# A hashed-attention kernel with two gated layers: the first head, the last head and the weight conversions dealt anew

## The chip, the cores and the metric

The program runs on one core of a Trainium2 chip. The metric is the time of one execution on the device in microseconds (us). The core has a TensorE (PE; its weight loads are a row of their own, PEld), a VectorE (DVE), a ScalarE (ACT), a GpSimd (POOL), a SyncE (SP) that here only issues DMAs, and DMA queues on SP and ACT. The engines run side by side and wait for each other through semaphores. A difference of over 0.3% of the time (2.2 us) is what a measurement of this kernel can tell.

## The reference, cut to what matters

```python
def _attn_ref(q, k, v, proj):                       # (2, 8, 768, 64) each, proj (64, 6)
    q_bits = (np.einsum('bhsd,dk->bhsk', q, proj) > 0)
    k_bits = (np.einsum('bhsd,dk->bhsk', k, proj) > 0)
    # bucket = sum(bits * 2**arange(6)); mask = q_bucket == k_bucket
    scores = scale * np.matmul(q, k.transpose(0, 1, 3, 2))
    scores = np.where(mask, scores, -1000000000.0)
    scores = scores - np.max(scores, axis=-1, keepdims=True)
    attn = np.exp(scores)
    attn = attn / (np.sum(attn, axis=-1, keepdims=True) + 1e-09)
    return np.matmul(attn, v)
# x = heads side by side, (1536, 512)
def _moe_ref(x, w_in, w_out):                       # w_in (512, 2048), w_out (2048, 512)
    h = x @ w_in
    return (h * np.tanh(np.log1p(np.exp(h)))) @ w_out
def _moe2_ref(x, w_in, w_out, a, b):
    h = x @ w_in
    P = a[0] + a[1] * h + a[2] * h**2 + a[3] * h**3
    Q = 1.0 + abs(b[0]) * abs(h) + abs(b[1]) * h**2
    return (P / (Q + 1e-06)) @ w_out
```

The three functions are applied one after the other. The weights of the two layers come as 64-bit floats, everything else as 32-bit floats.

## The kernel before, in words

**Precision.** Every large product is made from a rounded part ("hi") and a remainder ("lo"): `XH`, `XL`, `W[..][:, 0]`, `W[..][:, 1]`, `gh`, `gl`. A product is three: hi·hi, lo·hi, hi·lo. The lo parts are subtractions on VectorE (L73) or GpSimd (L70), the hi parts copies on ScalarE (L64) or GpSimd (L67).

**Attention.** 16 heads, one after the other, 768 queries by 768 keys, six key blocks `c` of 128. The bucket mask is folded into the score product: rows of codes (L328 to L341) stand under K and Q, and one more row holds each query's maximum. For that row `smax` (L392) multiplies six query blocks by all keys (two matmuls each, L398) and reduces each block on VectorE (L402). For all but head 0 the maxima are then transposed on VectorE (L410) and moved by a DMA of ACT's queue (`qB<-stt`, L415) into a row of `qB`; for head 0 matmuls with an identity (`row0`, L422) and two copies do it. Then `st` (L437) multiplies each key block by all queries (four matmuls, L446) and ScalarE takes the exponential of 128x768 (L451). `pair` (L471) adds exponentials two by two on GpSimd, `pv` multiplies by V (L293, 48 rows of the trace per head) and `dsum` (L481) adds the three sums of pairs with a matrix of ones. Two heads on, the divisors are gathered, inverted and spread by DMAs (L519, L531, L539), `norm` multiplies by them on VectorE (`xf`, L548), and `xhi`, `xlo` split the result for the layers.

**Order of the attention.** Each head has six slots. The table `order` in `attention` says in which slot a function of a head is called and, by the order of its lines, in which order the functions of one slot are; since each engine takes its instructions in program order, this sets the queues. The beginning is written out by hand (`start`). `warm(n)` issues n small matmuls on ones, whose result is not used. `two_banks` hands out four PSUM tiles in turn.

**Weights.** 64-bit floats become 32-bit by three integer operations on VectorE (L103, L106, L109), called a conversion below; then come hi and lo. Seven of the first layer's 16 feature tiles (`EARLY`) are converted during attention, in 14 parts, each split on GpSimd behind its conversion (`slot_split`). The other nine are converted in 36 parts over the steps of the first layer that `C1_AT` gives, and the second layer's later in the first layer; those are stored and read back as 32-bit words, and split from step n1-11 on (`split_at`).

**Dense part.** 96 steps: two layers, three blocks of 512 tokens, 16 feature tiles. A step is `gemm1` of one tile (12 matmuls, L731) and `gemm2` of an earlier one (12 matmuls, L749 or L751, of which four wait for `gl`), with the elementwise work of `front`, `recip`, `last`, `back` between. `tail(i)` puts the attention slots that remain behind the last head into steps 2, 3 and 5. Steps n1 (48) on belong to the second layer. `finish` writes the output, a tile of 128x512 per DMA.

Of the kernel before, what the change touches and what calls it, by code (L numbers as in the profile page):

```python
# [29 lines left out]
OLD = 3  # L30
EARLY = 7
# [7 lines left out]
C1_AT = 1, 14  # L39
# [8 lines left out]
def attention_moe_moe(ctx: ExitStack, tc: tile.TileContext, kq, v, proj2, cst, eye, w1, w2, ab, out):  # L48
# [110 lines left out]
    def attention(actx, tctx):  # L159
# [13 lines left out]
        turn = [0]  # L173
        ahead = []

        def two_banks():
            if ahead:
                return ahead.pop()
            turn[0] += 1
            return T[(turn[0] - 1) % 4]  # L180
# [20 lines left out]
        def memsets():  # L201
# [4 lines left out]
            for t in T:  # L206
                nc.vector.memset(t[:, :, HALF:HALF + 1], -BIG / 4)
# [24 lines left out]
        def load(h):  # L232
# [3 lines left out]
            if h == 0:  # L236
                home[0] = wpool.tile([128, 2, 2 * DM], F32, tag=f"w{EARLY - 1}", name="kq")
            raws[h] = home[0][:, h % 2, 0:S]
            nc.sync.dma_start(out=raws[h], in_=kq[b, hh])


# [17 lines left out]

        def khi(i):  # L260
            o = KK[0][64:128, i] if i < 2 else qX[0][0:64]
            nc.scalar.activation(out=o, in_=raws[0][0:64], func=ACT.Copy)

        def qhi():
            nc.vector.tensor_copy(qB[0][64:128], raws[0][64:128])
# [4 lines left out]
        def klo():  # L270
            lo_pool(qX[0][0:64], raws[0][0:64], qX[0][0:64])
# [42 lines left out]
        def codes(h):  # L314
            if not 0 <= h < OLD:
                return
            p = [two_banks() for _ in range(1 + (h == 0))]
            ct[h] = p[0][:, 0], p[-1][:, 1]
# [3 lines left out]
        def warm(n):  # L322
            if not ahead:
                ahead.append(two_banks())
            for _ in range(n):
                nc.tensor.matmul(out=ahead[0][0:32, 0, 0:128], lhsT=ones, rhs=wones, start=True, stop=True)
# [60 lines left out]
        def signs(h):  # L387
            for a in range(2):
                code_k(h, (a,))
                code_q(h, (1 - a,))  # L390

        def smax(h, c):  # L392
            if not 0 <= h < B * H:
                return
            p = two_banks()
            m = SM[h % 2][:, c:c + 1] if h else Z[:, 32 + c:33 + c]
            for a in range(2):
                nc.tensor.matmul(  # L398
                    out=p[:, a, 0:HALF], lhsT=qB[h % NB][:, c * 128:(c + 1) * 128], rhs=qhalf(KK[h % NB][:, 0], a),
                    start=True, stop=True,  # L400
                )
            nc.vector.tensor_reduce(out=m, in_=p[:, :, 0:HALF + 1], op=ALU.max, axis=AX.XY)  # L402
# [16 lines left out]
        def row0():  # L419
            p = two_banks()  # L420
            for c in range(NC):
                nc.tensor.matmul(  # L422
                    out=p[0:64, c // 3, c % 3 * 128:c % 3 * 128 + 128], lhsT=Z[:, c:c + 64], rhs=I_t,
                    start=True, stop=True,
                )
            nc.vector.tensor_copy(qhalf(qB[0], 1)[32:33], p[32:33, 1, 0:HALF])
            nc.scalar.activation(out=qhalf(qB[0], 0)[32:33], in_=p[32:33, 0, 0:HALF], func=ACT.Copy)
# [8 lines left out]

# [550 lines left out]
```

## Time and profile before

| | |
|---|---|
| time, median of 3 runs | 734.08 us (734.04 to 735.63) |
| the profiled execution | 734.39 us, of it 732.6 from the first instruction to the last |
| PE, PEld busy | 724.3 us (99%), 577.1 us (79%) |
| DVE, ACT, POOL busy | 575.9 us (79%), 416.4 us (57%), 130.3 us (18%) |
| DMA | 82.89 MB, mean 113 GB/s |

Durations in the rows come from that one profiled execution. PE's busy time counts matmuls that run at half the clock, and matmuls overlap, so 99% does not say that nothing could be shorter; what PE waits for stands in the waits and in the stretches. The attention takes the first 204 us, the first dense layer lies from 204 to 470, the second behind it. A row of the timeline joins like instructions of one engine that follow each other; its second number runs from the first one's start to the last one's end.

### The profile page before, as it was taken

The page shows a single profiled execution, that of the slowest core. Times are in us where ns is not written, and L with a number is a line of the kernel's source. Part 1 is how long each engine was busy: PE and PEld are TensorE (multiplying, and loading weights), DVE is VectorE, ACT ScalarE, POOL GpSimd, SP SyncE. Part 2 cuts the span into 40 slices and gives each one's busy share as a digit, 9 for nine tenths or more (in the row PEclk, how much of TensorE's full clock was granted, in tenths as well). Part 3 has the DMA queues.
Part 4 walks back from the last instruction along what each step waited for, and adds up shares of the span by engine and source line. Part 5 has one row for each costly group of instructions (what it writes and reads, how often), then busy time and mean ns, then how long its engine had stood idle before and what let it go on. Part 6 is the DMA issues. An engine that isn't in the chain of part 4 may idle for free.

```text
span 732.6 us, 11610 instructions
## 1 busy us (share of the span) xinstructions
PE 724.3 (99%) x4212; PEld 577.1 (79%) x4212; DVE 575.9 (79%) x1042; ACT 416.4 (57%) x688; POOL 130.3 (18%) x108
## 2 busy tenths in 40 slices
PE   8999999999999999999999999999999999999997
PEld 6777777676778788888888888878888888888886
DVE  6878898988568994655556876599998888898886
ACT  5766767676644432212122334687877767777674
POOL 7657566665700000000000000000000000000000
PEclk9999999999999999999999999999999999999999
DMA  5777868885144442455446884200001000010001
GB/s 156 207 205 191 224 183 215 192 213 141 35 129 137 146 138 78 151 165 172 145 151 203 275 251 156 86 1 1 0 1 57 1 1 0 1 58 0 1 1 58
DMA packets 48505, 82.89 MB, mean 113 GB/s; under 512 B 6634, under 2 KB 24256, under 8 KB 48448
## 3 DMA queue, kind: packets, MB, share of 16 engines
q1 hardware_dynamic: 48123, 82.07, 38.6%
q8 instruction: 33, 0.54, 0.3%
q14 instruction: 25, 0.20, 0.1%
q10 hardware_dynamic: 324, 0.08, 0.1%
HBM read 55.71 MB, written 14.14 MB: 95 GB/s over the span
## 4 chain that ended last, share of the span: by engine, by line
PE 83%; DVE 7%; DMA 5%; issue 1%; ACT 1%; POOL 1%; SPq 0%; POOLq 0%; ACTq 0%; DVEq 0%
PE h L731 31%; PE y L751 17%; PE y L749 15%; PE s L446 7%; PE s L293 6%; PE s L398 4%; PE s L481 1%; DMA d<-rc 1%; DMA qB<-stt 1%; DVE w L73 1%; DVE t L106 1%; DVE r L109 1%; DVE z L402 1%; DVE gl L73 1%; DMA R<-d 1%
## 5 line engine op out<-in xcount | busy, mean ns | idle before, releaser
L731 PE MATMUL h<-xh,w 128*128 128x512 f32 x768 | 204.9, 389 | 0.0
L731 PEld LDWEIGHTS h<-xh,w 128*128 128x128 f32 x768 | 144.2, 188 | 30.3 <-issue 0.3
L73 DVE TENSOR_TENSOR gl<-ep,gh 128x512 fp32r<-128x512 f32 x96 | 66.0, 687 | 70.8 <-ACT ep L775 70.1
L774 ACT ACTIVATE gh<-h 128x512 fp32r<-128x512 f32 x48 | 28.7, 598 | 149.4 <-PE h L731 136.3
L731 PE MATMUL h<-xl,w 128*128 128x512 f32 x384 | 102.6, 389 | 0.0
L402 DVE TENSOR_REDUCE smt<-s 128x1 fp32r<-128x770 f32 x90 | 86.4, 960 | 19.5 <-PE s L398 14.4
L751 PE MATMUL y<-w,gh 128*128 128x512 f32 x384 | 96.3, 389 | 0.0
L749 PE MATMUL y<-gh,w 128*128 128x512 f32 x384 | 94.8, 389 | 0.0
L471 POOL TENSOR_TENSOR es<-e,e 128x768 f32<-128x768 f32 x48 | 89.3, 1863 | 16.4 <-ACT e L451 15.1
L451 ACT ACTIVATE e<-s 128x768 f32<-128x768 f32 x96 | 77.3, 814 | 19.2 <-PE s L446 15.6
L731 PEld LDWEIGHTS h<-xl,w 128*128 128x128 f32 x384 | 72.1, 188 | 15.0
L749 PEld LDWEIGHTS y<-gh,w 128*128 128x128 f32 x384 | 72.1, 188 | 14.9
L751 PEld LDWEIGHTS y<-w,gh 128*128 128x128 f32 x384 | 72.1, 188 | 14.9
L293 PE MATMUL s<-e,vf 128*32 128x386 f32 x768 | 65.2, 488 | 0.0
L781 ACT ACTIVATE ep<-h 128x512 f32<-128x512 f32 x48 | 28.5, 595 | 52.3 <-PE h L731 52.3
L109 DVE SCALAR_TENSOR_TENSOR r<-r,t 128x256 int32<-128x256 int32 (+1 forms) x114 | 52.1, 457 | 4.8
L106 DVE SCALAR_TENSOR_TENSOR t<-r,t 128x256 int32<-128x256 int32 (+1 forms) x114 | 52.3, 458 | 3.9
L783 DVE TENSOR_TENSOR n<-n,ep 128x512 f32<-128x512 f32 x48 | 33.1, 690 | 26.7 <-ACT n L782 26.7
L751 PE MATMUL y<-w,gl 128*128 128x512 f32 x192 | 53.3, 392 | 0.5 <-DVE gl L73 0.4
L749 PE MATMUL y<-gl,w 128*128 128x512 f32 x192 | 51.6, 390 | 0.4 <-DVE gl L73 0.4
L446 PE MATMUL s<-qB,kk 128*128 128x384 f32 x192 | 50.5, 343 | 1.0 <-DMA qB<-stt 0.7
L293 PEld LDWEIGHTS s<-e,vf 128*32 128x32 f32 x768 | 24.7, 110 | 32.7 <-issue 30.3
(84 smaller groups left out, 991.1 us busy)
## 6 DMA issues: line engine op xcount, KB each, us to landing
r<-w SPq DMA_DIRECT2D x100, 256.0 KB
w<-r SPq DMA_DIRECT2D x64, 128.0 KB
w<-w SPq DMA_DIRECT2D x16, 512.0 KB
r<-w SPq DMA_DIRECT2D x14, 512.0 KB
kq<-kq SPq DMA_DIRECT2D x16, 384.0 KB
kk<-qB SPq DMA_DIRECT2D x15, 384.0 KB
kk<-qX SPq DMA_DIRECT2D x16, 192.0 KB
qX<-qB SPq DMA_DIRECT2D x16, 192.0 KB
```

Source lines behind the costliest of these rows:

```text
L73: nc.vector.tensor_tensor(out=o, in0=i, in1=f32(h), op=ALU.subtract)
L106: lambda: nc.vector.scalar_tensor_tensor(out=t, in0=r[:, :, 1], scalar=-0x40000000, in1=t, op0=ALU.bitwise_and, op1=ALU.bitwise_or),
L109: lambda: nc.vector.scalar_tensor_tensor(out=o, in0=r[:, :, 0], scalar=29, in1=t, op0=ALU.logical_shift_right, op1=ALU.bitwise_or),
L293: nc.tensor.matmul(out=o[32 * a:32 * a + 32, 0:HALF + 2], lhsT=w[:, a % 2 * 32:a % 2 * 32 + 32], rhs=x[:, a // 2], start=start, stop=stop,)
L402: nc.vector.tensor_reduce(out=m, in_=p[:, :, 0:HALF + 1], op=ALU.max, axis=AX.XY)
L446: nc.tensor.matmul(out=p[:, a, 0:HALF], lhsT=kk[:, c * 128:(c + 1) * 128], rhs=qq[:, a * HALF:(a + 1) * HALF], start=(i == 0), stop=(i == 1),)
L451: nc.scalar.activation(out=E[c][:, :, 0:HALF], in_=halves(p), func=ACT.Exp, scale=1.0 / D ** 0.5)
L471: nc.gpsimd.tensor_tensor(out=sums[h, c], in0=halves(pt[h, c]), in1=halves(pt[h, c + 1]), op=ALU.add)
L731: nc.tensor.matmul(out=p, lhsT=w[:, c * 128:(c + 1) * 128], rhs=x[:, c, :], start=(n == 0), stop=(n == 11))
L749: nc.tensor.matmul(out=y[m], lhsT=w[:, DM + m * 128:DM + (m + 1) * 128], rhs=g, **s)
L751: nc.tensor.matmul(out=y[m], lhsT=g[:, m * 128:(m + 1) * 128], rhs=w[:, DM:2 * DM], **s)
L783: nc.vector.tensor_tensor(out=v_, in0=v_, in1=u, op=ALU.mult)
```

## The change

Seven edits, all of them in the order or the engine of work, none in what is computed.

1. **Start.** Head 0's K and Q come in two DMAs of 384 columns (`load0`), and are rounded by halves (`khi0`, `qhi`). GpSimd writes the lo part of K at once where the scores read it, and ScalarE the second copy of Q's hi part (`qxhi`); two DMAs of 192 KB go. `row0(a)` makes the row of maxima for half of the queries, after three reductions each, with both copies on ScalarE. `st0(c, a)` makes head 0's scores by halves of the queries, 128x384 to an exponential. The first half stands among the reductions of head 0. Of 23 small matmuls (5+4+1+1+1+5+6) 9 are left (4+3+1+1).
2. **Weights beside the last heads.** A weight part's split that fell to the last head's slots is called in its last slot, behind its pairs.
3. **Last head.** VectorE adds the third pair, then folds the three sums into one (`fold`), and `dsum` has one part instead of three.
4. **Order table.** `norm` stands behind `weights`.
5. **First layer.** The 36 parts are dealt over steps 1 to 14 instead of 1 to 13. The late attention slots go to steps 6 and 7 instead of 5. Conversions by step from step 1 on were 3, 3, 3, 3, 2, 3, 3, 3, 2, 3, 3, 3, 2 and are 3, 3, 2, 3, 2, 3, 2, 3, 3, 2, 3, 2, 3, 2; the `xf` of the tail stands in the sixth of them, and stood in the fifth.
6. **Second layer's split.** Feature tiles 11 to 15 are split by halves, one in each of the steps n1 to n1+9, instead of two in each of n1 to n1+4.
7. **Output.** The last tile is negated in two halves, on ScalarE and VectorE, and leaves in two DMAs, of ACT's queue and of SP's.

```diff
-C1_AT = 1, 14
+C1_AT = 1, 15
+LATE_F = 11
...
+        def khi0(a):
+            nc.scalar.activation(out=qhalf(KK[0][64:128, 0], a), in_=qhalf(raws[0][0:64], a), func=ACT.Copy)
...
+        def qxhi():
+            nc.scalar.activation(out=qX[0][0:64], in_=f32(qB[0][64:128]), func=ACT.Copy)
...
         def klo():
-            lo_pool(qX[0][0:64], raws[0][0:64], qX[0][0:64])
+            lo_pool(KK[0][0:64, 1], raws[0][0:64], qX[0][0:64])
...
-            p = two_banks()
-            m = SM[h % 2][:, c:c + 1] if h else Z[:, 32 + c:33 + c]
+            p = T[2 - h + c % 2] if h < 2 else two_banks()
+            m = SM[h % 2][:, c:c + 1] if h else Z[:, 32 + 2 * c:33 + 2 * c]
...
+        def st0(c, a):
+            p = T[(0, 2 + a, 3 - 3 * a)[c // 2]][:, c % 2, 0:HALF]
+            for i in range(2):
+                nc.tensor.matmul(
+                    out=p, lhsT=KK[0][:, i, c * 128:(c + 1) * 128], rhs=qhalf((qB, qX)[i][0], a),
+                    start=(i == 0), stop=(i == 1),
+                )
+            pt[0, c] = E[c]
+            nc.scalar.activation(out=E[c][:, a, 0:HALF], in_=p, func=ACT.Exp, scale=1.0 / D ** 0.5)
...
-            nc.gpsimd.tensor_tensor(out=sums[h, c], in0=halves(pt[h, c]), in1=halves(pt[h, c + 1]), op=ALU.add)
+            eng = nc.vector if (h, c) == (B * H - 1, 4) else nc.gpsimd
+            eng.tensor_tensor(out=sums[h, c], in0=halves(pt[h, c]), in1=halves(pt[h, c + 1]), op=ALU.add)
+
+        def fold(h):
+            if h != B * H - 1:
+                return
+            for c in (4, 2):
+                nc.vector.tensor_tensor(out=sums[h, 0], in0=sums[h, 0], in1=sums.pop((h, c)), op=ALU.add)
...
-                jobs.setdefault(max(1, i + d), []).append((fn, p))
+                g = max(1, i + d)
+                jobs.setdefault(6 * nh - 1 if g >= 6 * nh - 6 else g, []).append((fn, p))
...
-            for g in {2: range(last, last + 5), 3: range(last + 5, last + 7), 5: range(last + 7, last + 30)}.get(i, ()):
+            for g in {2: range(last, last + 5), 3: range(last + 5, last + 7), 6: range(last + 7, last + 12),
+                      7: range(last + 12, last + 30)}.get(i, ()):
...
-                    split_at(n1 - NF + f + 5, 1, f, s, lo_dve)
+                    split_at(n1 + 2 * (f - LATE_F) + s if f >= LATE_F else n1 - NF + f + 5, 1, f, s, lo_dve)
```

First place: TensorE at the start, before, from the fifth block of head 0's maxima (L398 with `kk_138`) on. L326 are the small matmuls, L308 the codes of head 1, L422 the row of maxima, L446 head 0's scores.

```order
L398 MATMUL s_118<-kk_138,qB_132 128x384 x2
L326 MATMUL s_119<-wones,ones 32x128
L398 MATMUL s_119<-kk_138,qB_132 128x384 x2
L308 MATMUL s_116<-kq,pr 32x384 x4
L326 MATMUL s_117<-wones,ones 32x128 x5
L422 MATMUL s_117<-eye,z_128 64x128 x6
L326 MATMUL s_118<-wones,ones 32x128 x6
L446 MATMUL s_118<-qB_132,kk_138 128x384 x2
```

And now, from the same block (L405 with `kk_137`) on; L429 is the row of maxima, L446 now the scores by halves.

```order
L405 MATMUL s_117<-kk_137,qB_131 128x384 x2
L429 MATMUL s_116<-eye,z_127 34x128 x3
L405 MATMUL s_118<-kk_137,qB_131 128x384 x2
L446 MATMUL s_115<-qB_131,kk_137 128x384
L446 MATMUL s_115<-qX_134,kk_137 128x384
L446 MATMUL s_115<-qB_131,kk_137 128x384
L446 MATMUL s_115<-qX_134,kk_137 128x384
L446 MATMUL s_117<-qB_131,kk_137 128x384
```

The scores of the first half of the queries stand right behind the last block of maxima, and the small matmuls between are gone.

Second place: GpSimd at the end of the attention, before: the third sum of head 14, the last weight part's split (`w_2111`), and the last head's three sums.

```order
L471 TENSOR_TENSOR es<-e_102,e_103 128x768
L67 TENSOR_SCALAR w_2111<-r 128x512
L70 TENSOR_TENSOR w_2111<-r,w_2111 128x512
L471 TENSOR_TENSOR es<-e_98,e_99 128x768
L471 TENSOR_TENSOR es<-e_100,e_101 128x768
L471 TENSOR_TENSOR es<-e_102,e_103 128x768
```

And now, with the same weight part named `w_2105`:

```order
L491 TENSOR_TENSOR es<-e_101,e_102 128x768
L491 TENSOR_TENSOR es<-e_97,e_98 128x768
L491 TENSOR_TENSOR es<-e_99,e_100 128x768
L69 TENSOR_SCALAR w_2105<-r 128x512
L72 TENSOR_TENSOR w_2105<-r,w_2105 128x512
```

VectorE now, between the last conversion of the attention and the first `gl` of the dense part; before, only `xf` stood between these two.

```order
L111 SCALAR_TENSOR_TENSOR r<-r,t 128x512
L491 TENSOR_TENSOR es<-e_101,e_102 128x768
L497 TENSOR_TENSOR es<-es 128x768 x2
L574 TENSOR_TENSOR xf<-ev,R 128x768
L75 TENSOR_TENSOR gl<-ep,gh 128x512
```

The third sum and the two adds of `fold` are VectorE's, ahead of `xf`, and GpSimd's weight split stands behind its two sums.

Third place: VectorE in the second layer's first two steps, before; `w` is the lo part of a weight half.

```order
L73 TENSOR_TENSOR w_4606<-w_4606 128x512 x2
L759 TENSOR_TENSOR xl_71<-y,xh_68 128x512 x4
L799 SCALAR_TENSOR_TENSOR ep<-ep,ab 128x512
L800 SCALAR_TENSOR_TENSOR n<-n,ep 128x512
L801 SCALAR_TENSOR_TENSOR ep<-n,ep 128x512
L783 TENSOR_TENSOR n<-n,ep 128x512
L785 TENSOR_TENSOR ep<-ep,h 128x512
L786 SCALAR_TENSOR_TENSOR ep<-ep,ab,h 128x512
L73 TENSOR_TENSOR w_4643<-w_4643 128x512 x2
L73 TENSOR_TENSOR gl<-ep,gh 128x512
```

And now:

```order
L75 TENSOR_TENSOR w_4594<-w_4594 128x512
L797 TENSOR_TENSOR xl_71<-y,xh_68 128x512 x4
L845 SCALAR_TENSOR_TENSOR ep<-ep,ab 128x512
L846 SCALAR_TENSOR_TENSOR n<-n,ep 128x512
L847 SCALAR_TENSOR_TENSOR ep<-n,ep 128x512
L829 TENSOR_TENSOR n<-n,ep 128x512
L831 TENSOR_TENSOR ep<-ep,h 128x512
L832 SCALAR_TENSOR_TENSOR ep<-ep,ab,h 128x512
L75 TENSOR_TENSOR w_4594<-w_4594 128x512
L75 TENSOR_TENSOR gl<-ep,gh 128x512
```

One lo part stands ahead of `xl` and of `gl` where two stood, in this and in the steps that follow.

## Rows read from the trace of the kernel before

**Rows 1.** Waits of the span: engine line waited for: us in total, times, longest.
```profile
PEld y L751 <- DVE gl L73: 2.2, 4, 0.8
...
PEld y L749 <- DVE gl L73: 1.2, 2, 0.9
...
PEld s L481 <- POOL es L471: 0.8, 1, 0.8
...
PE s L446 <- DMA qB<-stt: 0.7, 2, 0.5
```

**Rows 2.** Timeline, start: start, us, engine line op, out<-in xcount [idle before].
```profile
1.17 2.34 PE L326 MATMUL s<-wones,ones 128*32 128x128 f32 x10 [1.17 <-DVE s L207]
...
8.33 5.29 DVE L402 TENSOR_REDUCE z<-s 128x1 fp32r<-128x770 f32 x6 [1.07 <-PE s L398]
...
12.18 1.25 PE L326 MATMUL s<-wones,ones 128*32 128x128 f32 x10
...
14.93 1.37 DVE L332 TENSOR_SCALAR kk<-s,cst 13x384 fp32r<-13x384 f32 x2
...
15.67 0.62 PE L446 MATMUL s<-qB,kk 128*128 128x384 f32 x2
...
17.02 6.16 DVE L402 TENSOR_REDUCE smt<-s 128x1 fp32r<-128x770 f32 x6 [0.71 <-PE s L398]
...
23.11 4.07 PE L293 MATMUL s<-e,vf 128*32 128x386 f32 x48
...
28.08 0.62 PE L446 MATMUL s<-qB,kk 128*128 128x384 f32 x2
```

**Rows 3.** Chain of waits, 24 to 80 us: start, us, what.
```profile
36.57 3.41 DMA qB<-stt
```

**Rows 4.** Timeline, 150 to 170 us: ACT queue, TensorE.
```profile
155.29 0.68 ACTq L415 DMA_DIRECT2D qB<-stt  x1
...
159.05 0.59 PE L446 MATMUL s<-qB,kk 128*128 128x384 f32 x2 [0.38 <-DVE t L106]
```

**Rows 5.** Timeline, end of the last head.
```profile
194.81 4.33 ACT L451 ACTIVATE e<-s 128x768 f32<-128x768 f32 x6
...
195.83 1.29 POOL L70 TENSOR_TENSOR w<-r,w 128x512 fp32r<-128x512 f32 x1
...
196.90 1.03 DVE L548 TENSOR_TENSOR xf<-ev,R 128x768 f32<-128x768 f32 x1 [1.86 <-DMA R<-d]
...
197.08 6.15 POOL L471 TENSOR_TENSOR es<-e,e 128x768 f32<-128x768 f32 x3
...
202.04 0.83 PE L481 MATMUL s<-es,ones 128*32 128x192 f32 x16
...
203.28 0.53 PE L481 MATMUL s<-es,ones 128*32 128x192 f32 x8 [0.41 <-POOL es L471]
```

**Rows 6.** Chain of waits, 190 to 230 us.
```profile
197.12 2.52 POOL es L471
...
213.30 0.60 DVE gl L73
...
218.53 0.60 DVE gl L73
```

**Rows 7.** Timeline, VectorE in the first dense layer.
```profile
230.06 0.29 DVE L103 TENSOR_SCALAR t<-r 128x256 int32<-128x256 int32 x1 [1.33 <-DMA r<-w]
...
235.18 0.95 DVE L548 TENSOR_TENSOR xf<-ev,R 128x768 f32<-128x768 f32 x1
```

**Rows 8.** Timeline where layer two begins.
```profile
477.25 1.29 DVE L73 TENSOR_TENSOR w<-w 128x512 fp32r<-128x512 f32 x2
...
482.95 1.98 PE L751 MATMUL y<-w,gh 128*128 128x512 f32 x8
...
488.74 1.97 PE L751 MATMUL y<-w,gh 128*128 128x512 f32 x8
```

**Rows 9.** Busy time by stretch: stretch, us, each engine (instructions), clock, DMA share, GB/s.
```profile
499.00:728.00 229.00, 229.00 (x1012) 189.63 (x1011) 201.74 (x307) 166.76 (x261) 0.00 (x0) 1.00 0.03 10
```

**Rows 10.** Timeline, end of the program.
```profile
728.97 0.69 DVE L763 TENSOR_SCALAR o<-y 128x512 f32<-128x512 f32 x1 [0.67 <-PE y L751]
```

More of the change, by code (lines that the diff above doesn't have):

```diff
@@ L30 @@
 OLD = 3
+UP = 124
 EARLY = 7
@@ L316, in codes @@
                 return
-            p = [two_banks() for _ in range(1 + (h == 0))]
-            ct[h] = p[0][:, 0], p[-1][:, 1]
+            if h == 0:
+                ct[h] = T[0][:, 0], T[1][:, 1]
+            elif h == 1:
+                ct[h] = T[1][:, 0], T[1][:, 0]
+            else:
+                p = two_banks()
+                ct[h] = p[:, 0], p[:, 1]
             code_products(h)
         def warm(n):
-            if not ahead:
-                ahead.append(two_banks())
             for _ in range(n):
-                nc.tensor.matmul(out=ahead[0][0:32, 0, 0:128], lhsT=ones, rhs=wones, start=True, stop=True)
+                nc.tensor.matmul(out=T[0][0:32, 1, 0:128], lhsT=ones, rhs=wones, start=True, stop=True)
         def code_k(h, of=(0, 1)):
@@ L384, in quad_in @@
                 )
[L387 to L390, printed above, removed]
         def smax(h, c):
@@ L475, in dsum @@
                 return
-            parts = [sums.pop((h, c)) for c in PAIRS] + [pt[h, c] for c in range(2 * len(PAIRS), NC)]
+            parts = [sums.pop((h, c)) for c in PAIRS if (h, c) in sums] + [pt[h, c] for c in range(2 * len(PAIRS), NC)]
             p = two_banks()
@@ L619, in attention @@
             ("store", store, 17, 0),
-            ("norm", norm, 23, 0),
             ("xlo", xlo, 29, 0),
             ("weights", weights, 0, -1),
+            ("norm", norm, 23, 0),
             ("gather", gather, 12, 0),
@@ L678, in run @@
             fns = {o[0]: o[1] for o in order}
-            fns.update(get=get, coef=coef, khi=khi, qhi=qhi, qlo=qlo, klo=klo, signs=signs, row0=row0, ident=ident, spare=spare)
-            done.update((name, (0,)) for name in ("hi", "lo", "move_k", "code_ka", "code_kb", "code_q", "fin_b"))
+            fns.update(
+                get=get, coef=coef, khi=khi, khi0=khi0, qhi=qhi, qxhi=qxhi, qlo=qlo, klo=klo, row0=row0, ident=ident,
+                spare=spare, st0=st0, load0=load0, table=table, code_qa=lambda h: code_q(h, (0,)),
+                code_qb=lambda h: code_q(h, (1,)),
+            )
+            done.update((name, (0,)) for name in ("load", "hi", "lo", "move_k", "move_x", "move_h", "fin_b"))
+            done.update(("code_q", (h,)) for h in (0, 1))
             for name, *k in start:
```

67 lines of the change are left out of this document (40 added, 27 removed).

## The prediction

> **What bounds the kernel now.** I read the busy times first: PE 724.3 of 732.6 us. So I looked for where PE waits, or works at half its clock, and asked of each edit which of these places it touches. The waits of the span name the places: VectorE's `gl` holds PE's weight loads in both layers, 2.2 us in four waits and 1.2 in two, GpSimd's sum of pairs holds them 0.8 once at the last head, and the DMA of the row of maxima (`qB<-stt`) holds PE 0.7 in two waits [rows 1]. The timeline of the start shows the largest place, in which PE is busy by its record and yet ahead of nothing: the first score is at 15.67, behind six reductions of 5.29 us that start at 8.33 [rows 2]. Between 499 and 728 us PE has no gap: 1012 matmuls in 229.00 us, 0.226 each, so a step of 24 is 5.43 us [rows 9]. Nothing outside these places can give time.
>
> **Start.** Three limits follow each other. First, the reductions of head 0 on VectorE: 5.29 / 6 = 0.88 each. The halves of the load and the shorter roundings let them start up to 0.3 us before 8.33; I take 8.05, so the third ends at 10.7 and the sixth at 13.35. Twelve of head 0's 24 score matmuls then run beside reductions 4 to 6 and need no place of their own. Second, the reductions of head 1. Before, they start at 17.02: behind `code_k(1)` (14.93 + 1.37) come 0.72 us of matmul and hand-over. Now: 13.35 + 1.37 + 0.72 = 15.45. Before, they were fed by PE, which had head 0's scores between them: 6.16 / 6 = 1.03 each. Now PE has half of these scores left, and VectorE's own 0.88 binds. The sixth began at 17.02 + 5 x 1.03 = 22.15, and `pv` of head 0 0.96 behind it, at 23.11; now the sixth begins at 15.45 + 5 x 0.88 = 19.85 and `pv` at some 20.4 to 20.8, which is 2.3 to 2.7 earlier [rows 2]. Third, head 1's first score, at 28.08 before, 4.97 behind `pv`: so 25.4 to 25.8 by PE. It also needs the row of maxima: reductions over at 20.75, transposes about 0.9 (four small operations before as now), then a DMA of 3.41 [rows 3], 25.1 in all. PE is just later. ScalarE gets twelve exponentials of half size for six whole ones; the whole ones follow each other at 4.33 / 6 = 0.72 [rows 5], the half ones are not in the trace, so they cost between 0.36 (all of it columns) and 0.72 (none of it): the last six of them 2.2 to 4.3 us, from about 14.6 on, done by 19 at the latest, ahead of `pv`. The removed 192 KB moves stood on SP ahead of loads, and nothing gets later by their going. I take -2.3, for the ties with the DMA and ScalarE; bounds -1.3 (the DMA 0.3 longer, ScalarE late by one exponential, no gain from the half load) and -2.9 (all limits at their earliest).
>
> **The two waits for the row, and `norm`.** The row of maxima still comes behind the same chain of DMAs per head at 40 and 64 us, and its 0.7 stays: 0. At 159.05 PE waits 0.38, and the row names a conversion (L106), beside which `norm` stands. But the row DMA was issued at 155.29, and with 3.41 it lands at 158.7, within 0.35 of that matmul [rows 3, 4]. So moving `norm` behind the conversion gives nothing here; with the other reading it gives 0.4. I take 0, bounds -0.4 and +0.2 (`norm` before the reductions costs 0.95 [rows 7] where VectorE is late).
>
> **Last head.** Before: six exponentials from 194.81 to 199.14, GpSimd's weight split until 197.12, then three sums until 203.23, the last of which PE needs at 203.28 for its last eight sums [rows 5]. Alone a sum is (6.15 - 2.52) / 2 = 1.82; the first took 2.52 and stood beside VectorE's `xf` (196.90, 1.03) [rows 5, 6]. Now GpSimd's sums start when their exponentials are there, 196.3 and 198.15, and end at 200.0. VectorE has the third from 199.25 and two folds behind it, each as `xf`, 0.95 [rows 7]. With no hindrance: 199.25 + 2.85 = 202.1, and the eight matmuls at 202.2 instead of 203.28, -1.1 (no earlier in any case than 202.04, when `pv` ends). If VectorE's adds have to wait for GpSimd's second sum and then run through: 202.85, -0.35. If GpSimd's moved split (0.62 and 1.29; the latter at 195.83 in [rows 5]) gets in between them: +0.6 for one, 204.8 for both, +1.5. I take 0, between the last two; bounds -1.1 and +1.5. The `xf` behind the folds comes some 6 us later than before; its reader is the tail, steps later.
>
> The row shows 2.52 for a sum beside a two-input operation of VectorE and 1.82 without. The Trainium skill, page "SBUF — State Buffer", section "Who interferes with whom", says that a VectorE instruction with two inputs in SBUF and a GpSimd instruction that reads SBUF exclude each other for a whole instruction, and that who comes first has it. The row agrees: 197.94, when `xf` ends, and 1.82 make 199.76, against 199.64 measured. By that rule the -1.1 falls away and what is left is which of the two gets in, -0.35 to +1.5.
>
> **First layer.** A step with three conversions is a chain on VectorE of 5.23 (213.30 to 218.53), of which `gl` is about 0.69, so a conversion with its lo part is 1.51 [rows 6]. Against PE's 5.43 such a step gains 0.2. Before, the third step has `recip` and two `xl` besides (taken by their size like `gl`, 1.5 in all) and is some 1.4 over; the fifth has two conversions, `xf` (0.95) and two `xl` and is 0.6 over; and a DMA is late by 1.33 at 230.06 [rows 7]. Together 3.3, of which two waits of 1.2 come through to PE [rows 1]; the rest was lead. Of a wait of a weight load about 0.1 costs PE nothing (below), so the stall is 0.9 to 1.0. Now the third step has two conversions (even), the fifth two (1.5 of lead gained), the sixth `xf` (0.75 over), the seventh two `xl` and two conversions (even). Even with the DMA late by 1.33 the lead holds: -0.9, bounds -0.3 (if the later tail makes another DMA late by 1.5) and -0.9. The conversions still end before the second block needs them.
>
> **Second layer's first steps.** There a step takes 488.74 - 482.95 = 5.79, 0.36 over 5.43, and VectorE's chain is its cause: two lo parts among it, 1.29 from the first's start to the second's end, each 0.69 long like `gl`, so 0.6 from start to start [rows 8, 9]. With one the chain is 5.2, below PE's step. The four waits are 2.2 in all, the longest 0.8, so the other three 0.47 each [rows 1], where the step is 0.36 longer: 0.1 of a wait costs nothing, and the four cost 1.7. Step n1 loses one lo ahead of `xl` and one ahead of `gl`, 1.29, more than its longest wait of 0.8. The halves moved to steps n1+5 to n1+9 meet chains of 4.6 us plus 0.6, under 5.43. -1.7, bounds -1.4 and -1.75.
>
> **End.** VectorE's last copy (728.97, 0.69) [rows 10] becomes two halves side by side, 0.3 shorter at most, but a second DMA queue's latency ends then: -0.05, between -0.3 and +0.2.
>
> **Sum.** -2.3 + 0 + 0 - 0.9 - 1.7 - 0.05 = -4.95. The profiled execution took 734.39 (span 732.6 and 1.8 around it), so 729.4; it lies 0.3 over the median, which makes 729.2.
>
> **Rivals.** *A: the start is given back.* Each head depends on DMAs of the one before (rows of maxima, codes, loads), and two waits for the row at 40 and 64 us (0.5 the longer [rows 1]) show that this chain is hardly ahead of PE. If it doesn't move forward with PE, PE waits 2.3 longer there: 731.5. For it: the row DMA and PE tie at 25 us by my working. Against it: the chain starts from the same reductions, which come earlier, and removed DMAs only free the queue. *B: GpSimd's split gets between the folds.* +1.5: 730.7. For it: the first sum was delayed beside `xf`; against it: VectorE has its next add ready at once. *C: the folds are not hindered*, -1.1: 728.1; the 2.52 speaks against it. *D, slower: the clock.* Ten small matmuls took 2.34 at 1.17 us and 1.25 at 12.18 [rows 2]: the first at TensorE's lower level (1.2 GHz), the second at the upper (2.4). 14 of the 23 small matmuls that keep PE busy before 15.6 are gone. If the level rises only when the stream of real scores is under way, the 36 score and maximum matmuls from 15.67 on (six to each 1.03, 6.2 us) take twice that. From 29 of them (5 us) on the change is no gain, and with all 36 the time is 735.4. Against it: the matmuls ahead of 7 us are nearly as many as before, and from 11 us real scores stand where small matmuls stood.
>
> The Trainium skill, page "TensorE: Matmul & The Clock Gate", Part 1, section "What's actually happening", says that the slow clock is the default and activity releases it. That speaks against taking small matmuls out, and is D; the rows agree in so far as the first matmuls are the slow ones.
>
> **Chances.** Forecast, with terms inside their bounds, 0.6; A 0.17; B 0.1; C 0.09; D 0.04. 0.3% of the time is 2.2 us, which is about what a measurement of this kernel can tell from no change. Faster by more, below 731.9: the forecast, B, C and most of A, 0.86. Within it: the rest of A, and A with B, 0.1. Slower: D, 0.04. The range runs from 727.3 (start -2.9, folds -1.1, the rest as forecast) to 732.2 (A with some of B).
>
> **What would show it.** First score at about 11.6 and first score of head 1 at 25.4 to 25.8; PE's waits for `gl` in both layers gone, and steps of 5.43 from 478 us on; the third sum on VectorE starting when GpSimd's second ends, and the last `dsum` matmuls at 203 or a little later; the waits at 40, 64 and 159 shifted by the start's gain and as long as before. I am wrong if head 1's first score gains and a head later the gain is gone (A), if the first matmuls behind 12 us still last twice as long (D), or if waits for `gl` only move to later steps.

## The result and the profile after

The changed kernel took 740.34 us (median of six runs, 737.68 to 742.12), the kernel before 734.19 beside it: a ratio of 1.0073 [1.0059, 1.0087], slower by 0.7%. The forecast was 729.2, with a range to 732.2. The profiled execution of after took 737.68 (span 735.7, mean granted clock 1.000); three of the other five had a mean clock of 0.993 and took 739.7 to 740.8, one took 740.4 at 0.998. So two things are to be explained: 3.1 us more span at full clock, and some 2.7 us more in most executions.

TensorE's waits in after (us in total, times, longest), which answer to [rows 1]:

```profile
PE s L446 <- ACT e L451: 3.6, 6, 1.0
PE s L507 <- DVE es L497: 2.0, 1, 2.0
...
PE s L338 <- ACT qB L353: 1.0, 1, 1.0
PE s L465 <- ACT dv L536: 1.0, 1, 1.0
PE s L465 <- DMA qB<-stt: 0.9, 3, 0.5
```

None of these but the last stood there before. All waits of PE for `gl` are gone. The start in the timeline (start, us, engine line op, [idle before]), which answers to [rows 2]:

```profile
7.95 1.65 PE L405 MATMUL s<-kk,qB 128*128 128x384 f32 x4
...
9.06 1.83 DVE L409 TENSOR_REDUCE z<-s 128x1 fp32r<-128x770 f32 x2 [2.49 <-PE s L405]
...
11.33 3.59 DVE L409 TENSOR_REDUCE z<-s 128x1 fp32r<-128x770 f32 x4 [0.44 <-PE s L405]
...
13.80 0.44 PE L446 MATMUL s<-qB,kk 128*128 128x384 f32 x1
...
15.00 0.44 PE L446 MATMUL s<-qB,kk 128*128 128x384 f32 x1 [0.58 <-ACT e L451]
...
17.03 0.34 PE L429 MATMUL s<-eye,z 128*34 128x128 f32 x3
...
18.26 1.35 DVE L344 TENSOR_SCALAR kk<-s,cst 13x384 fp32r<-13x384 f32 x2 [3.35 <-ACT qB L433]
...
18.80 0.44 PE L446 MATMUL s<-qB,kk 128*128 128x384 f32 x1 [1.02 <-ACT e L451]
...
20.33 0.96 DVE L409 TENSOR_REDUCE smt<-s 128x1 fp32r<-128x770 f32 x1 [0.71 <-PE s L405]
...
26.88 4.07 PE L302 MATMUL s<-e,vf 128*32 128x386 f32 x48
...
31.86 0.62 PE L465 MATMUL s<-qB,kk 128*128 128x384 f32 x2
```

The first score is 1.9 earlier than before (13.80 for 15.67; it was forecast at about 11.6), and everything behind it is later: `pv` of head 0 by 3.77, the first score of head 1 by 3.78. Between 15 and 25 us PE stands six times, 3.6 us in all, for an exponential that reads the tile it wants to write. The two longest waits (1.02 and 0.91) stand where ScalarE has another piece ahead of that exponential, a copy of 0.48 or a rounding of 0.84.

Head 1's reductions start 4.88 later than forecast (20.33 for 15.45). Of this, 1.57 is that head 0's reductions end at 14.92 instead of 13.35, and 3.35 is VectorE's idle time ahead of head 1's codes (18.26). The codes wait for the copy of the second half of the row of maxima, which has a part of their tile, and the matmuls of this row (L429, 17.03) stand in PE's queue behind the scores that wait.

The last head, which answers to [rows 5]:

```profile
198.52 0.62 PE L465 MATMUL s<-qB,kk 128*128 128x384 f32 x2 [0.96 <-ACT dv L536]
...
202.89 4.10 PE L302 MATMUL s<-e,vf 128*32 128x386 f32 x48
...
204.02 1.71 DVE L491 TENSOR_TENSOR es<-e,e 128x768 f32<-128x768 f32 x1 [5.22 <-ACT e L470]
...
204.88 1.33 POOL L69 TENSOR_SCALAR w<-r 128x512 fp32r<-128x512 f32 x1
...
205.83 3.12 DVE L497 TENSOR_TENSOR es<-es 128x768 f32<-128x768 f32 x2
...
206.29 1.84 POOL L72 TENSOR_TENSOR w<-r,w 128x512 fp32r<-128x512 f32 x1
...
209.00 0.53 PE L507 MATMUL s<-es,ones 128*32 128x192 f32 x8 [2.01 <-DVE es L497]
...
209.46 1.20 PE L769 MATMUL h<-xh,w 128*128 128x512 f32 x4
```

Two losses stand here: the head's first score waits 0.96 for a copy of `dv` (this `pv` is 4.77 later than before, 1.0 more than the start's loss), and from `pv` to the first matmul of the dense part it takes 6.57 instead of 5.63. The two adds of `fold` take 3.12 (1.18 and 1.83, with gaps), while the weight split, which falls right upon them, takes 1.33 and 1.84 instead of 0.62 and 1.29.

The dense part, which answers to [rows 8]; the second fence is busy time by stretch, columns as in [rows 9]:

```profile
481.61 1.98 PE L789 MATMUL y<-w,gh 128*128 128x512 f32 x8
```

```profile
470.00:500.00 30.00, 30.00 (x134) 24.82 (x134) 27.23 (x43) 25.48 (x41) 0.00 (x0) 1.00 0.08 29
```

PE has no gap from 470 to 500, and the step is 5.44. From its first matmul to the end of the span the dense part takes some 526.3 instead of 528.9. The same second-layer matmul stood at 476.83 before, 273.08 behind the first dense one, and now 272.15 behind it; from there to the last matmul it takes 250.01 instead of 251.71. So -0.93 and -1.70, as forecast. These two hold beyond this pair of profiles: the second stretch is 250.01 or 250.02 in all eleven profiles of this document that have the dense edits, and 251.71 or 251.72 in the four that don't. The first is 272.13 to 272.18 in eight of the eleven (the other three follow further down) and 273.08 to 274.75 in the four.

The end. The two halves of the last tile were to be negated side by side; VectorE's half waits for ScalarE's:

```profile
732.47 0.42 DVE L804 TENSOR_SCALAR o<-y 128x256 f32<-128x256 f32 x1 [1.08 <-ACT o L803]
```

Sum of the profiled executions: +3.77 (start) + 1.0 (`dv`) + 0.94 (last head) - 0.93 - 1.70 + 0.05 (end) = +3.1, the whole difference of the spans.

### The profile page after: what moved, and what is told of

Same layout as the page of the kernel before. It is cut to its first block, busy times and chain, and to the rows that moved or that the text cites. A ratio compares the mean times of both kernels' runs of the same rounds, so it can differ in the third digit from the quotient of the medians.

```text
span 735.7 us, 11526 instructions
## 1 busy us (share of the span) xinstructions
PE 721.7 (98%) x4168; PEld 573.8 (78%) x4168; DVE 579.8 (79%) x1045; ACT 417.3 (57%) x698; POOL 132.5 (18%) x107
## 4 chain that ended last, share of the span: by engine, by line
PE 93%; DMA 3%; DVE 2%; ACT 2%; issue 1%; DVEq 0%; SPq 0%; ACTq 0%
PE h L769 36%; PE y L789 18%; PE y L787 18%; PE s L465 8%; PE s L302 6%; PE s L405 4%; DMA qB<-stt 1%; PE s L507 1%; DMA qX<-qB 1%; PE s L446 1%; ACT e L470 1%; PE s L365 1%; ACT e L451 0%; PE s L317 0%; DVE es L497 0%
## 5 line engine op out<-in xcount | busy, mean ns | idle before, releaser
L491 POOL TENSOR_TENSOR es<-e,e 128x768 f32<-128x768 f32 x47 | 86.8, 1848 | 24.2 <-ACT e L470 23.5
L470 ACT ACTIVATE e<-s 128x768 f32<-128x768 f32 x90 | 72.7, 815 | 18.7 <-PE s L465 16.7
L405 PE MATMUL s<-kk,qB 128*128 128x384 f32 x192 | 50.1, 343 | 0.0
```

The source lines that it names most:

```text
L405: nc.tensor.matmul(out=p[:, a, UP:UP + HALF], lhsT=qB[h % NB][:, c * 128:(c + 1) * 128], rhs=qhalf(KK[h % NB][:, 0], a), start=True, stop= ...
L470: nc.scalar.activation(out=E[c][:, :, 0:HALF], in_=halves(p), func=ACT.Exp, scale=1.0 / D ** 0.5)
L491: eng.tensor_tensor(out=sums[h, c], in0=halves(pt[h, c]), in1=halves(pt[h, c + 1]), op=ALU.add)
```

## The experiments

Three theories for the start. *W*: the exponentials of half size and TensorE take turns on shared PSUM tiles. *F*: the small matmuls that were removed held the clock and the pace of the start. *R*, for the last head's wait: the new start leaves another count in the rotation of PSUM tiles. Ratios are to the kernel before, which ran beside each version.

**The changed kernel again.**

> The changed kernel once more, for its spread and its clock. Theory W (waits): head 0's half scores share a two-bank tile by pairs, so the second block's matmuls wait for the first block's exponential, and this and nothing else costs the start 3.8 us; the executions above 737.7 us are those in which TensorE's idle time at 13 to 25 us lets its clock fall, so their mean granted clock is below 0.995 and their time 2 to 4 us above. Theory F (filler): it is the 14 small matmuls taken out that make the clock late, and the waits cost little. Both expect 738 to 742 and a mean clock that falls as the time rises; a time of 742 at a clock of 1.0 would speak against both.

Measured: 738.85 (736.86 to 742.97), ratio 1.0065 [1.0041, 1.009]. The same kernel's two medians are 1.5 apart (740.34 and 738.85); differences "against after" below are to this second one. This time the profiled execution was one at a lower clock (742.97, mean 0.991). By stretch (PE, PEld, DVE, ACT, POOL; then granted clock, DMA share, GB/s):

```profile
12.00:16.00 4.00, 2.58 (x11) 1.42 (x11) 1.46 (x2) 2.62 (x6) 1.52 (x6) 0.91 0.55 204
16.00:20.00 4.00, 2.95 (x10) 2.29 (x11) 1.34 (x2) 1.88 (x4) 0.00 (x0) 0.50 0.52 147
20.00:24.00 4.00, 3.50 (x11) 2.99 (x10) 1.35 (x2) 2.19 (x5) 2.28 (x2) 0.50 0.34 70
```

And the last two of these stretches in after's first profile, which is at 1.00 in all of them:

```profile
16.00:20.00 4.00, 2.40 (x13) 1.75 (x13) 1.33 (x2) 2.55 (x7) 0.00 (x0) 1.00 0.55 147
20.00:24.00 4.00, 2.87 (x15) 2.26 (x14) 2.76 (x3) 2.39 (x6) 3.20 (x2) 1.00 0.50 105
```

In the first profile PE is busy 2.40 of 4 us at 16 to 20, where before has 4.00. In the second it is granted half its clock (1.2 GHz) for these eight microseconds, and `pv` of head 0 starts at 28.91 instead of 26.88. The clock fell while PE was waiting for exponentials, and not in every execution; the six runs go from 736.86 at a mean clock of 1.0 to 742.97 at 0.991. Time and clock do not go strictly together, though both theories expected it: one run took 740.58 at 0.997, another 738.87 at 0.992.

The start differs in one more thing. In this profile the first four matmuls of head 0's maxima took 0.97 instead of 1.65, and the first reduction began at 8.07 instead of 9.06:

```profile
7.35 0.97 PE L405 MATMUL s<-kk,qB 128*128 128x384 f32 x4
...
8.07 4.42 DVE L409 TENSOR_REDUCE z<-s 128x1 fp32r<-128x770 f32 x5 [1.45 <-PE s L405]
```

The profile gives the granted clock as 1.00 in both from 0 to 12 us. So the first reduction can start 1 us apart in two executions of one kernel, and the granted clock does not show it.

**The old start with all other edits.**

```diff
-UP = 124
...
-        def st0(c, a):
...
-            ("st0", 4, 0), ("st0", 5, 0), ("hi", 2), ("lo", 2), ("move_k", 2), ("coef",),
+            ("move_k", 2), ("warm", 6), ("st", 0, 0), ("coef",),
```

> The start of the kernel before, with all other edits of the change. By the two traces the change's later parts are worth -2.6 in the dense layers, +0.9 at the last head (the folds) and +1.0 for a wait of the last head's first score on a tile that the divisor copy still reads. Theory W: the last of these hangs on the start too, since the start sets where the rotation of the four tiles stands, so it goes: 734.2 - 2.6 + 0.9 = 732.5 (732.1 to 733). If that wait comes from the late attention slots instead: 733.5. Rival (the start is not the cause, the moves in the dense part are): 737 or more.

Measured: 734.43 (732.99 to 736.16), 0.9997 [0.9987, 1.0007]: 1.9 above the 732.5 that was expected, but 4.4 below after, and the wait for `dv` is gone with the new start. The wait for the folds stays at 2.0.

**The new start alone, in before.** The opposite diff.

> The new start alone, with everything else as before. Theory W: first score of head 1 at 31.9 instead of 28.1, +3.8, and +1.0 at the last head's first score, and on top of it 0 to 4 where the clock is late: 738 to 743, mean clock below before's 0.999. Rival (the start is not the cause): 734 to 735. The two rows to look at are the first score of head 1 and the wait ahead of the last head's first score.

Measured: 740.95 (740.51 to 744.48), 1.0096 [1.007, 1.0122]: the start alone loses more than the whole change does. Its profile was at full clock, with `pv` of head 0 at 26.61 and

```profile
PE s L445 <- ACT e L450: 3.6, 6, 1.0
...
PE s L464 <- ACT dv L528: 1.0, 1, 1.0
```

**Scores of two blocks ahead of their two exponentials.** `st0` puts two key blocks into the two banks of one PSUM tile, and this kernel's semaphores order whatever touches a tile. Here the four matmuls of a tile come first, then its two exponentials; nothing else is moved.

```diff
-            for i in range(2):
...
+            for d in (c, c + 1):
+                p = T[(0, 2 + a, 3 - 3 * a)[c // 2]][:, d % 2, 0:HALF]
+                for i in range(2):
...
+            for d in (c, c + 1):
...
+                nc.scalar.activation(out=E[d][:, a, 0:HALF], in_=p, func=ACT.Exp, scale=1.0 / D ** 0.5)
```

> The changed kernel, with the matmuls of both key blocks of a pair written ahead of the two exponentials that read their tile; same instructions, same tiles, same sizes. Theory W: the six waits of TensorE for the exponentials (3.6 us, longest 1.0) go except for what ScalarE's own rate leaves, head 1's first score comes 1.5 to 3.5 us earlier than 31.9, and the time falls to 734.5 to 736.5, with less spread and a higher clock. Theory F and a ScalarE that is simply too slow for twelve half exponentials (0.49 each) both expect no gain over 0.7 us.

Measured: 735.56 (734.09 to 737.01), 1.0011 [1.0001, 1.0022], so -3.3 against after. From its timeline:

```profile
14.36 1.64 ACT L456 ACTIVATE e<-s 128x384 f32<-128x384 f32 x4 [0.45 <-PE s L449]
...
18.60 5.40 DVE L409 TENSOR_REDUCE smt<-s 128x1 fp32r<-128x770 f32 x6 [0.71 <-PE s L405]
...
23.76 4.07 PE L302 MATMUL s<-e,vf 128*32 128x386 f32 x48
```

PE's waits for exponentials are gone, and `pv` is 3.1 earlier than in after's first profile (0.7 of it is that head 0's reductions end at 14.19 instead of 14.92). W is shown. (The Trainium skill, page "PSUM — Partial Sum Buffer", section "PSUM bank collisions raise a hardware error", asks for guards by bank and quadrant of partitions; the kernel's tiles guard two banks at once. No run here has PE write one bank of a tile while ScalarE reads the other.) `pv` is still 0.65 later than before: head 1's codes and the second half of the row are late, as below.

**Without the folds.** The third sum is GpSimd's again and `dsum` has three parts; the split stays where after has it.

```diff
-            eng = nc.vector if (h, c) == (B * H - 1, 4) else nc.gpsimd
-            eng.tensor_tensor(out=sums[h, c], in0=halves(pt[h, c]), in1=halves(pt[h, c + 1]), op=ALU.add)
...
-            ("fold", fold, 5, 1),
```

> The changed kernel with the last head's three sums of pairs back on GpSimd and three parts in the last dsum, the weight split still behind them. Theory L (port): the folds cost 1.3 us, since VectorE's two-input adds and GpSimd's two weight instructions take turns; without folds GpSimd's third sum ends as pv ends and the sums' matmuls start at once: first dense matmul 5.2 us behind the last head's pv instead of 6.6, the 2.0 us wait of TensorE for the fold gone, 737.5. Rival (the extra matmuls of three parts and GpSimd's third sum cost what the folds cost): no difference over 0.4 us, 738.8.

Measured: 737.03 (736.22 to 739.96), 1.0034 [1.0021, 1.0048], 1.8 below after.

```profile
205.02 5.84 POOL L490 TENSOR_TENSOR es<-e,e 128x768 f32<-128x768 f32 x3 [6.28 <-ACT e L470]
```

From `pv` of the last head to the dense part it is 5.0 (206.67 to 211.67), and no wait for sums is left: GpSimd has no split ahead of its three sums. So the moved split alone gains 0.6 (5.0 for 5.63), and with the folds on top it becomes a loss of 0.94.

The folds can cost more than that. Five profiles have the 2.0 us wait for them: after, the changed kernel again, the old start, the pairs of scores, and the rotation dealt out (below). In three of these the granted clock is lower right behind the wait. The lines are of the changed kernel again, the pairs of scores and the rotation dealt out:

```profile
212.00:216.00 4.00, 3.27 (x15) 2.38 (x16) 1.55 (x2) 1.87 (x3) 0.00 (x0) 0.66 0.72 235
...
204.00:208.00 4.00, 2.62 (x14) 1.83 (x15) 2.19 (x2) 2.53 (x4) 0.51 (x1) 0.76 0.57 188
...
208.00:212.00 4.00, 3.93 (x16) 2.96 (x17) 0.88 (x2) 1.70 (x2) 0.00 (x0) 0.57 0.67 216
```

In these three the second layer starts 273.72 to 273.76 behind the first dense matmul instead of 272.13 to 272.18, 1.6 more. In the ten profiles without so long a wait there, the clock does not fall at the dense part's beginning.

**The old start and no folds**, the two edits above together.

> Old start and no folds: what is left are the weight split behind the last head's sums, norm behind the weights, the dense moves and the output in halves. By the sum of the runs so far: 734.4 - 1.3 = 733.1, 1.0 to 1.9 under the kernel before. If the terms do not add (the dense layers' 2.6 us are given back to something else when the start is old): 734.4 and up.

Measured: 732.08 (731.09 to 732.8), 0.9959 [0.9945, 0.9974]: 1.0 below the 733.1 that was expected, at mean clocks of 0.999 to 1.0. The expectation priced the folds at 1.3; what the clock can lose behind them was not in it.

**The folds, with the weight split back ahead of the pairs.**

```diff
-                g = max(1, i + d)
-                jobs.setdefault(6 * nh - 1 if g >= 6 * nh - 6 else g, []).append((fn, p))
+                jobs.setdefault(max(1, i + d), []).append((fn, p))
```

> The changed kernel with the folds, but the last weight split where it was before, ahead of the last head's sums on GpSimd, so that GpSimd has nothing behind its second sum. Theory L: the two folds take 1.9 us (0.95 each) instead of 3.1, and the last dsum starts 1.3 earlier against the last head's pv: 4.8 instead of 6.1 behind it. Rival (VectorE's adds are slow for another reason, such as their tiles): 3.1 us and 6.1 as before.

One execution, 738.76 (mean clock 0.993). From its last head:

```profile
208.13 2.02 DVE L497 TENSOR_TENSOR es<-es 128x768 f32<-128x768 f32 x2
...
210.21 0.53 PE L507 MATMUL s<-es,ones 128*32 128x192 f32 x8 [0.83 <-DVE es L497]
```

With GpSimd idle beside them the two adds take 2.02 instead of 3.12, and PE waits 0.83 instead of 2.01. From `pv` to the dense part it is 5.38: the folds alone gain 0.25 against before, as the split alone gains 0.6, and it is the two together that lose.

**Before, without 14 of its small matmuls.**

```diff
-            ("move_h", 0), ("load", 2), ("smax", 0, 2), ("warm", 1), ("move_x", 1), ("smax", 0, 3), ("warm", 1),
+            ("move_h", 0), ("load", 2), ("smax", 0, 2), ("move_x", 1), ("smax", 0, 3),
...
-            ("move_k", 2), ("warm", 6), ("st", 0, 0), ("coef",),
+            ("move_k", 2), ("st", 0, 0), ("coef",),
```

> The kernel before, without 14 of its 23 small matmuls (those behind the first maxima), nothing else changed. Theory F (filler): without them the granted clock falls in the stretch from 8 to 20 us, mean clock 0.99 to 0.995, and the time grows by 2 to 4 us, 736 to 739. Theory W: the clock falls where TensorE stands idle for long, which the old start does less; the time grows by under 1 us, 734 to 735.5, at a mean clock of 0.997 or more.

Measured: 738.74 (737.19 to 739.88), 1.0053 [1.0036, 1.007], at mean clocks of 0.993 to 0.997. So F holds too, for before: matmuls whose results nobody reads are worth 3.7 us there.

```profile
12.00:16.00 4.00, 1.74 (x10) 1.62 (x11) 3.20 (x5) 1.64 (x4) 1.85 (x7) 0.83 0.87 245
...
16.00:20.00 4.00, 4.00 (x19) 3.99 (x18) 2.45 (x4) 3.20 (x5) 2.64 (x2) 0.75 0.58 166
```

PE is busy 1.74 of 4 us at 12 to 16, and the next stretch is granted 0.75. In this one profile the start is only 0.6 later for it (`pv` at 23.71; the other profiles of the old start have it at 22.87 to 23.48), and the rest comes as later waits, for `gl` and for DMAs. How the 3.7 divides in the other executions is not shown.

**All that is sound, the start mended.** Pairs of scores as above; no folds; the row of maxima in another tile than head 1's codes; these codes ahead of the second half of the row; five small matmuls in an unused tile for three that waited for `qB`; one piece of head 1's Q codes (`code_qa`) a little later; and the tile rotation dealt out (below).

```diff
-            p = T[1][:, 1]
+            p = T[0][:, 1]
...
-            ("st0", 0, 0), ("st0", 1, 0), ("st0", 2, 0), ("st0", 3, 0), ("row0", 1), ("code_ka", 1), ("code_kb", 1),
+            ("st0", 0, 0), ("st0", 1, 0), ("st0", 2, 0), ("st0", 3, 0), ("code_ka", 1), ("code_kb", 1), ("row0", 1),
```

> The changed kernel with its start repaired: matmuls of a pair ahead of its exponentials, head 0's row of maxima on the tile of the scores that need it anyway instead of head 1's codes' tile, head 1's codes on VectorE ahead of that row, five small matmuls ahead of the first maxima on a tile nobody reads; no folds; three heads each skip one tile of the rotation, so that the last head needs no jump of three. Theory W with L: all that kept the forecast of the start from coming true are waits on shared tiles, so pv of head 0 comes at 20.5 to 21.5 (23.1 before, 26.9 in the change), and of that lead 1.5 to 2.3 arrive at the end: 729.5 to 731, 1 to 2.5 under the 732.1 of the old start without folds. Rival G (given back: the DMA chain of the maxima's rows limits the heads anyway): pv of head 0 early, but 732 in all.

Measured: 730.57 (729.89 to 731.28), 0.9941 [0.9927, 0.9954]. The time is as expected, the way to it isn't: `pv` of head 0 was expected at 20.5 to 21.5 and is at 23.05.

```profile
7.32 1.65 PE L405 MATMUL s<-kk,qB 128*128 128x384 f32 x4
...
14.35 1.35 DVE L344 TENSOR_SCALAR kk<-s,cst 13x384 fp32r<-13x384 f32 x2
...
17.34 0.85 PE L405 MATMUL s<-kk,qB 128*128 128x384 f32 x4
...
17.89 5.41 DVE L409 TENSOR_REDUCE smt<-s 128x1 fp32r<-128x770 f32 x6 [2.19 <-PE s L405]
...
23.05 4.07 PE L302 MATMUL s<-e,vf 128*32 128x386 f32 x48
```

Head 1's codes are there at 15.7, but its first maxima stand in PE's queue behind scores that wait for the second half of the row.

**The dense edits alone, in before.**

```diff
-C1_AT = 1, 14
+C1_AT = 1, 15
+LATE_F = 11
...
-                if i == 5:
+                if i == 7:
```

> The kernel before with the dense part's edits alone (conversions over 14 steps, late slots at steps 6 and 7, second layer's halves one a step). The forecast gave -0.9 and -1.7, together -2.6, and the traces agree between the first dense matmul and the end: 732.4 (732 to 732.9). Rival (a part of the stalls depends on when DMAs land and stays, or comes elsewhere): 733.5 to 734.5.

Measured: 732.41 (732.06 to 733.69), 0.997 [0.996, 0.9981], as expected.

**After, with the rotation dealt out.** The last head skips PSUM tiles until the count fits; here one tile is skipped in each of heads 12 to 14 instead.

```diff
+            if c == 0 and h in (12, 13, 14):
+                turn[0] += 1
             while (h, c) == (B * H - 1, 0) and turn[0] % 4 != 2:
```

> The changed kernel, with the jump of three tiles ahead of the last head dealt out as one tile at each of heads 12, 13 and 14. If the wait of 0.96 us ahead of the last head's first score comes from the tile that the sums of the head before have just used, it goes, and the last head's first score starts 1.1 behind those sums' matmuls instead of 2.1. If it comes from ScalarE being late: it stays at about 1.

One execution, 738.16.

```profile
197.59 0.62 PE L467 MATMUL s<-qB,kk 128*128 128x384 f32 x2
...
201.98 4.10 PE L302 MATMUL s<-e,vf 128*32 128x386 f32 x48
```

The wait ahead of the last head's first score is gone; from `pv` to `pv` it is 9.39, as before, instead of 10.40. R is shown. (A wait of 0.46, for the copy to `ev`, stands ahead of an earlier head's score instead, at 162.87.)

**`norm` moved alone, in before.**

```diff
-            ("norm", norm, 23, 0),
             ("xlo", xlo, 29, 0),
             ("weights", weights, 0, -1),
+            ("norm", norm, 23, 0),
```

> The kernel before with norm behind the weights in the order table, nothing else. The forecast was 0 (the row DMA ends the wait at 159 us, not VectorE): 734.4 to 735.2, the same as the kernel before within 0.4. The other reading of that row (a conversion ends it): -0.4 for each place of that kind.

Measured: 734.72 (733.72 to 736.94), 1.0001 [0.9991, 1.0012].

**The mended start, with head 1's first maxima ahead of the waiting scores.**

```diff
-            ("st0", 4, 0), ("st0", 5, 0), ("hi", 2), ("lo", 2), ("move_k", 2), ("coef",),
+            ("row0", 1), ("smax", 1, 0), ("smax", 1, 1), ("hi", 2), ("lo", 2), ("move_k", 2), ("coef",),
```

> The repaired kernel, with head 1's first two blocks of maxima on TensorE ahead of the second half of head 0's scores, and the third pair of the first half ahead of the second row of maxima. Theory Q (queue): the repaired start only ties with the old one, since head 1's first maxima stand behind scores that wait for the second row's copy, and VectorE idles 2.2 us ahead of its first reduction of head 1 (17.9); with them in front that reduction starts at 16.3 to 16.6, pv of head 0 comes at 21.3 to 22 instead of 23.05, and the time is 729.2 to 730 instead of 730.6 if the lead arrives at the end. Rival G (given back): pv of head 0 early, but the wait for the row DMA ahead of head 1's or 2's first score takes it: 730.6. Rival R (ScalarE's twelve half exponentials are the bound): pv of head 0 stays at 23.

Measured: 730.58 (729.56 to 732.46), 0.9947 [0.9926, 0.9967].

```profile
7.02 0.97 PE L405 MATMUL s<-kk,qB 128*128 128x384 f32 x4
...
13.08 1.35 DVE L344 TENSOR_SCALAR kk<-s,cst 13x384 fp32r<-13x384 f32 x2
...
15.13 1.83 DVE L409 TENSOR_REDUCE smt<-s 128x1 fp32r<-128x770 f32 x2 [0.70 <-PE s L405]
...
18.07 3.56 DVE L409 TENSOR_REDUCE smt<-s 128x1 fp32r<-128x770 f32 x4 [1.11 <-PE s L405]
...
21.50 4.07 PE L302 MATMUL s<-e,vf 128*32 128x386 f32 x48
```

`pv` of head 0 is 1.6 earlier than before, and in the profiled executions the span is 1.6 shorter than that of the mended start (727.9 for 729.5). Most of that is luck of the executions: up to head 1's codes the two kernels have the same order, and yet these start at 13.08 here and at 14.35 there: head 0's reductions end at 13.03 and 14.29, behind first matmuls that took 0.97 and 1.65. From the codes to `pv` it is 8.42 here and 8.70 there, so the edit itself is worth 0.3 in this pair: the 2.19 of VectorE's idle time are 0.70 now, but 1.11 come back ahead of its third reduction. The medians are equal, over five runs each, which fits. Both versions beat before by 0.5 to 0.6%.

## Why the prediction was wrong

- **Start: -2.3 forecast, +3.77 measured; this step failed.** It said that twelve scores "run beside reductions 4 to 6 and need no place of their own", took VectorE from head 0's last reduction to head 1's first with 1.37 + 0.72 between, and had ScalarE's half exponentials done by 19. That counted each engine's work and no hand-over. With two blocks in one tile, block 2's scores wait for block 1's exponential and the reverse, six waits of 3.6 in all; the second half of the row stands behind these scores in PE's queue, head 1's codes wait for its copy, and head 1's maxima for the codes. So VectorE's reductions of head 1 start at 20.33 instead of 15.45, and the last half exponential begins at 25.64. The half exponentials themselves took 0.49 alone and 0.41 to 0.44 in a row, inside the bounds of 0.36 to 0.72. The first reduction was late by 1.0 in this profile (9.06 for 8.05); in the changed kernel's other profile it began at 8.07, as forecast.
- **Rotation of tiles: no term forecast, +1.0.** The prediction did not ask which tile the last head's first score gets. [rows 5] shows no wait there, and the diff of `two_banks` was in view.
- **Last head: 0 forecast, +0.94 measured, inside -1.1 to +1.5.** Rival B was right in kind: the split gets between the folds. Not forecast were the 1.6 that the dense part loses in three of five profiles in which the clock is lower behind the folds' wait. The rows show a 3.12 beside a busy GpSimd and 2.02 beside an idle one. The Trainium skill, page "SBUF — State Buffer", section "Who interferes with whom", has a VectorE instruction with two SBUF inputs and a GpSimd one that reads SBUF exclude each other, and whoever issues first goes first; the two rows agree. The argument against B, that VectorE "has its next add ready at once", did not hold: the split's first operation was issued at 204.88, during VectorE's third sum, and its second at 206.29, during the first fold (205.83 to 207.01), and the second fold took 1.83.
- **First layer -0.9 and second layer -1.7: -0.93 and -1.70.** Right, by the same working, and again with the dense edits alone (732.41 of 734.83, -2.4).
- **`norm` and the end: 0 and -0.05.** `norm` was right (1.0001). The end's number was inside its bounds (+0.05), its mechanism was not: the halves were to run "side by side", and VectorE's half waited 1.08 for ScalarE's, as in the start two engines on shared tiles. From the last matmul to the end of the span it is 4.1 to 4.7 in the fifteen profiles, with the edit and without, so no gain shows.
- **Clock: rival D, held at 0.04, was partly right.** Its place, the matmuls from 15.67 on, is where the clock fell in one of after's two profiles (0.50 from 16 to 24 us) and in that of before without small matmuls (0.75 from 16 to 20). The argument "from 11 us real scores stand where small matmuls stood" rested on the step that failed: PE had waits there instead. With these waits taken out, and as few small matmuls, the clocks are 0.997 to 1.0 (pairs of scores; the fall in its profile is the one behind the folds) and 0.999 to 1.0 (mended start, without folds). In six of the fifteen profiles the granted clock falls, and each time PE had just stood in waits, of this start, of the folds, or where small matmuls were missing. After's first profile has the same waits at a clock of 1.00, so waits alone do not decide it; what does is not shown. One reading of D is weaker than it looks: the first ten small matmuls are slow by their duration alone (2.34 for 1.25); the profile gives the granted clock as 1.00 there.
- **Rival A** had no gain to give back in the changed kernel. In the last experiment's profile the lead over the mended start is 1.6 at head 0's `pv` and still 1.8 at that of the last head (196.44 for 198.20), so it was not given back there.

How the executions at lower clock lose their 2 to 5 us can be followed in one profile, that of 742.97 against that of 737.68: 2.0 by head 0's `pv`; 1.7 in the heads, where two first scores wait 0.92 and 1.38 (one such wait is 1.44 in the old start without folds, at full clock, so these are not the clock's); and 1.6 behind the folds. For the executions without a profile it stays open.

## What to carry to other kernels

When work is cut in halves, list for each piece the tile it shares and with whom, and lay out the hand-overs one by one; a rate per engine is a bound only where the queue ahead of the engine does not wait. Ask of each engine's queue, in order, what stands behind an instruction that waits. And before matmuls that compute nothing are taken out, show that PE has no idle time in that place without them.

## What the runs showed of the hardware that was not expected

- The same kernel had the stretch from 16 to 24 us at a granted clock of 1.00 in one execution and 0.50 in another, and its runs go from 736.86 to 742.97. One wait of 2.0 us was followed by a lower clock in three profiles of five, at 1.6 us each.
- The first four matmuls of head 0's maxima took 1.65 in one execution and 0.97 in another, both at a granted clock of 1.00 by the profile.
- An exponential over 128x384 takes 0.49 alone and 0.41 in a row, where 128x768 takes 0.72 in a row: halves cost ScalarE 14% more in sum (0.82 for 0.72), and in after PE stood 3.6 us for them besides.
- Beside VectorE's adds the weight split's first operation took 1.33 instead of 0.62: what the two engines lose to each other shows as longer instructions and in no row of waits.
